# First feed-forward product: longer planned transfers, two raw buffers per matrix, relu stores issued by ScalarE, narrowing that begins on ScalarE

## The chip, the cores and the metric

One core of a Trainium2 chip. A core has TensorE (PE: matmuls; PEld is its loading of weights), VectorE (DVE), ScalarE (ACT), GpSimd (POOL) and SyncE (SP), each with a queue that runs in order, and 16 DMA engines that move data between HBM and the on-chip memory. Here nearly all transfers are issued from SP's queue. The metric is the time of one execution in device microseconds.

## The reference, cut to what matters

Attention (4 x 12 heads, 448 positions, 64 wide) feeds a gated convolution block, and that feeds a normalized feed-forward block; 4 x 448 = 1792 rows of 768 in all.

```python
xn = (x - mu) / np.sqrt(var + 1e-06) * g_ln
ch = np.maximum(xn @ w_ch1, 0.0) @ w_ch2     # 768 -> 3072 -> 768
return (x + ch).astype(np.float32)
```

`w_ch1` and `w_ch2` are float64 arrays. The kernel gets them as pairs of 32-bit words and narrows them to float32 on the chip.

## The kernel before, in words

**Phases.** Attention and gate come first (to about 254 us in the profile), then the output projection with the normalization (to about 355), then the first feed-forward product (355 to 737) and the second (from 737 to the end). The change lies in the first feed-forward product, in the two narrowings done ahead of it, and in the buffers that the second takes over.

**Precision.** Each float32 operand is split into a high part, rounded to the fast matmul type (F32R), and a low part, the rest. Each product is three matmuls: high x high, high x low, low x high.

**The first product.** `w_ch1` is cut into NJ = 24 column blocks of 128, the rows into NM = 4 row blocks (one of 256 rows, three of 512). A unit (j, m) is 18 matmuls into one of three PSUM banks (ring `c`). `ch1_products` (L589) issues them. Units run j by j; the last `LASTJ` blocks are run row block by row block instead. When a unit is done, `keep` (L880) has ScalarE write its relu into one of four buffers (`r1`), and a DMA stores that to `hd` in DRAM (L888, 96 stores).

**The weights of the first matrix.** `w1_steps` (L810) makes block j: load the raw words into ring `raw0` (one buffer), narrow them into `wt`, scale by `g_ln` (L240), ScalarE casts the high part into a slot of ring `w1` (five slots `blk`), VectorE subtracts to get the low part (L819). `first_steps` (L691) does the same for blocks 0 and 1 in the phase before.

**The second matrix beside it.** Its 24 raw pieces are narrowed in the same stretch, two per step, 12 steps in all (`w2_steps`, L828). The two pieces go from ring `raw1` (two buffers) into the one tile `comb`; four VectorE operations form sums and differences (L847), ScalarE casts the high parts into `combh` (L856), VectorE subtracts the low parts (L858), and two DMAs of 1344 KB store both tiles to `wd` in DRAM (L862, L863). The second product loads from `hd` and `wd` and takes over `X`, `blk`, `comb`, `combh`, `relu` and the raw buffers as space.

**Narrowing one piece** (`narrowing`, L791; 128 x 768 float64). Load (L792); three VectorE steps build the float32 bits from the two words (L220, L222, L224); ScalarE takes the absolute value of the high word, read as a float (L233), and writes it over the low word; a fourth VectorE step sets small values to zero (L236).

**What sets the order.** All of it is put in order before the kernel runs. `Plan.arrange` (L99) is a list scheduler: each task has a cost in ns on its engine, a `lag` after which its result is there (for DMAs), a due time, the tasks it comes after, and the buffers it takes. At any planned moment it starts, on each free engine, the earliest due among those tasks whose predecessors and buffers are ready; tasks are not held back until they are due. The result is one fixed order per engine. On the chip each engine runs its list in that order and waits, at the head of its queue, for whatever the next instruction needs. Planned costs of units are 4104 ns (512 rows) and 2160 ns (256 rows), `ENDB` is their sum. A block of the first matrix is due 22 us before its first unit, and 10 us before the next block.

The lines of the narrowing's load and of its due time:

```python
ld = task({"SP": 1500}, lambda e: nc.sync.dma_start(out=raw.tile, in_=src), due - 8,
          [raw_last[raw.tag], *need], [raw], lag=3000)
```

`need` is, for the second matrix, the last subtraction of the step before (`lo_last`).

Of the kernel before, what the change touches and what calls it, by code (L numbers as in the profile page):

```python
# [16 lines left out]

MIN_HIGH = 3.4332275390625e-05
# [139 lines left out]
def f32(ap):  # L158
    return ap.bitcast(F32)
# [3 lines left out]
def attention_gate_ffn(  # L163
# [71 lines left out]
    def narrow_2(raw, w):  # L235
        nc.vector.scalar_tensor_tensor(w, f32(raw[:, :, 0]), MIN_HIGH, w, ALU.is_ge, ALU.mult)  # L236

# [337 lines left out]
    NX = 2  # L575
# [6 lines left out]
    with ExitStack() as ph2:  # L582
# [13 lines left out]

        with ExitStack() as ph2a, tc.manual_schedule():
# [93 lines left out]
            def first_steps(n):  # L691

                raw, w, dst = Buf("wraw"), Buf("wt"), {}
# [3 lines left out]
                def bits(i):  # L697
                    def fn(e):
                        if i == 0:
                            dst["ops"] = narrow_ops(raw.tile, w.tile)  # L700
                        next(dst["ops"])
                    return fn

                k = ld
                for i, ns in enumerate((590, 990, 875)):
                    k = task({"DVE": ns}, bits(i), due + 0.01 * i, [k], [w] if i == 0 else [], [raw] if i == 0 else [raw, w])
                k = task({"ACT": 815}, lambda e: narrow_abs(raw.tile), due + 0.2, [k], [], [raw])
                def last(e):
                    narrow_2(raw.tile, w.tile)
                    scale_rows(w.tile)  # L710

                k = task({"DVE": 1740}, last, due + 0.3, [k], [], [raw, w])
# [15 lines left out]
        with ExitStack() as ph2b, tc.manual_schedule():  # L728
            bp = ph2b.enter_context(tc.tile_pool(name="bp", bufs=1, reuse_waits="tile"))
            ps_b = ph2b.enter_context(tc.tile_pool(name="ps_b", bufs=1, space=PSUM, reuse_waits="tile"))  # L730
            blk += [bp.tile([P, 2, DM], F32R, name=f"w1_{i}") for i in (2, 3, 4)]
            raws = [wr.tile([P, DM, 2], U32, tag="wraw", name="wraw")]
            raws += [bp.tile([P, DM, 2], U32, name=f"wraw{i}") for i in (1, 2)]
# [18 lines left out]
            def as_h(t, at):  # L752
# [3 lines left out]
                "raw0": raws[:1], "raw1": raws[1:], "w1": blk, "wt": [bp.tile([P, DM], F32, name="wt")], "comb": [comb], "combh": [combh],  # L756
# [5 lines left out]
                + [as_h(blk[s], i * NH) for s in (2, 3) for i in range(2)] + [as_h(X[3], 2 * NW + i * NH) for i in range(2)]  # L762
                + [as_h(blk[4], i * NH) for i in range(2)],
                "S": [cut(t, 0, 4 * JJ * P, i=4, j=JJ) for t in (comb, relu)],
                "r": [cut(f32(t), 0, 4 * JJ * P, f=2, j=JJ) for t in map(f32, raws)],
# [4 lines left out]
            LASTJ = 3  # L770
# [15 lines left out]
            w1_buf, w1_ready, w1_last, raw_last, lo_last = {}, {}, [None], {"raw0": None, "raw1": None}, [None]  # L786
# [4 lines left out]
            def narrowing(src, w_of, due, new, w_buf, raw, need=()):  # L791
                ld = task({"SP": 1500}, lambda e: nc.sync.dma_start(out=raw.tile, in_=src), due - 8, [raw_last[raw.tag], *need], [raw], lag=3000)  # L792
                raw_last[raw.tag] = ld
                dst = {}

                def bits(i):
                    def fn(e):
                        if i == 0:
                            dst["ops"] = narrow_ops(raw.tile, w_of())
                        next(dst["ops"])  # L800
                    return fn

                k = ld
# [277 lines left out]
```

## Time and profile before

| | |
|---|---|
| median of 3 runs | 1049.47 us (1048.47 to 1050.14) |
| profiled execution | 1049.6 us |
| its span, first to last instruction | 1047.9 us |
| TensorE busy in the span | 1004.5 us, 96 % |
| VectorE busy | 748.8 us, 71 % |
| ScalarE busy | 472.4 us, 45 % |
| GpSimd busy | 318.6 us, 30 % |
| TensorE clock, mean granted | 0.992 |
| moved by DMA | 193.76 MB |

How to read it: a busy share is a mean over the phases of the span, and TensorE's busy time is that of pipelined matmuls, so a busy engine may still run at the lower clock or wait to refill. What matters for a phase is which wait ends last there. Granted clock is that of TensorE, 1.00 being 2.4 GHz. In rows with "<-", the operation left of it waited for the one to its right; "SPq" and "ACTq" are the queues of SP and ScalarE, where DMA issues stand, which are not counted as busy. "Landing" is the time from a DMA's issue to its last data.

### The profile page before, as it was taken

Reading aid. Unit: us, or ns where it says so; the run is one execution under the profiler, and the core shown is the slowest. Engines: PE = TensorE matmul, PEld = TensorE weight load, DVE = VectorE, ACT = ScalarE, POOL = GpSimd, SP = SyncE. Lnnn points to the kernel's source line nnn. Section 1 sums busy time; section 2 is a strip of 40 time slices with the busy share of each in tenths; the row PEclk is TensorE's granted clock in tenths of the full one; section 3 lists DMA queues with packets and bytes.
Section 4 is the critical chain, followed back from the end, with each engine's and each line's share of the span. In section 5 each row is a group of like instructions: output and inputs, shape, how many; then the busy total and the mean of one; then the engine's idle time right before and its main releaser. Section 6 shows DMA issues by size and latency. Waiting matters only on the chain.

```text
span 1047.9 us, 16248 instructions
## 1 busy us (share of the span) xinstructions
PE 1004.5 (96%) x5947; PEld 882.5 (84%) x5947; DVE 748.8 (71%) x1361; ACT 472.4 (45%) x958; POOL 318.6 (30%) x389
## 2 busy tenths in 40 slices
PE   9989899999999999999988988899999999999998
PEld 5657677779999988878777876678999999999998
DVE  7898889763744467877767778761697787777773
ACT  8897878851554334434333343332333333333330
POOL 6979869560100000000000000001564443433510
PEclk9999999999999999999999999999999999999999
DMA  6354454332321367776777766679725616626422
GB/s 203 102 180 158 138 169 150 106 92 86 119 62 46 99 223 235 263 254 239 254 276 279 246 226 246 233 274 395 277 91 194 273 61 231 237 69 253 161 106 91
DMA packets 94127, 193.76 MB, mean 185 GB/s; under 512 B 8800, under 2 KB 75360, under 8 KB 90464
## 3 DMA queue, kind: packets, MB, share of 16 engines
q1 hardware_dynamic: 93904, 192.73, 52.4%
q8 instruction: 47, 0.77, 0.3%
q14 instruction: 32, 0.26, 0.1%
q10 hardware_dynamic: 144, 0.00, 0.0%
HBM read 126.65 MB, written 66.06 MB: 184 GB/s over the span
## 4 chain that ended last, share of the span: by engine, by line
PE 63%; DVE 17%; DMA 13%; POOL 3%; issue 2%; SPq 1%; ACT 0%; DVEq 0%; ACTq 0%; POOLq 0%
PE bank L998 23%; DMA wraw<-in_w_ch 13%; PE bank L594 12%; PE o L639 8%; PE val L554 5%; PE e L998 4%; PE t L399 2%; PE pv L423 2%; PE s L554 2%; DVE g L441 2%; DVE comb L847 2%; DVE wt L222 2%; PE s L328 2%; DVE wt L224 2%; POOL p L364 2%
## 5 line engine op out<-in xcount | busy, mean ns | idle before, releaser
L594 PE MATMUL bank<-x,w 128*128 128x512 f32 (+1 forms) x1692 | 355.5, 372 | 27.0 <-ACT relu L885 25.0
L594 PEld LDWEIGHTS bank<-x,w 128*128 128x128 f32 x1692 | 296.3, 192 | 85.8 <-ACT relu L885 31.3
L949 POOL TENSOR_TENSOR comb<-wraw 128x384 f32<-128x384 f32 x28 | 33.1, 1184 | 428.6 <-DMA hd<-relu 362.7
L1009 DVE TENSOR_TENSOR acc<-bank,acc 128x384 f32<-128x384 f32 x168 | 93.1, 554 | 71.7 <-PE bank L998 71.5
L998 PE MATMUL bank<-x,w 128*128 128x384 f32 x657 | 121.1, 334 | 0.0
L233 ACT ACTIVATE wraw<-wraw 128x768 f32<-128x768 f32 x60 | 55.6, 930 | 136.2 <-DVE comb L222 92.7
L998 PEld LDWEIGHTS bank<-x,w 128*128 128x128 f32 x657 | 114.5, 188 | 0.0
L364 POOL TENSOR_SCALAR p<-p,r 128x128 f32<-128x128 f32 (+1 forms) x144 | 78.1, 562 | 21.5 <-DVE r L360 13.8
L998 PE MATMUL bank<-x,x 128*128 128x384 f32 x432 | 81.6, 334 | 0.2 <-DVE acc L1009 0.2
L356 ACT ACTIVATE p<-p,negm 128x128 f32<-128x128 f32 (+1 forms) x144 | 71.8, 503 | 11.1 <-DVE negm L350 10.5
L998 PEld LDWEIGHTS bank<-x,x 128*128 128x128 f32 x432 | 75.4, 188 | 0.5 <-issue 0.5
L441 DVE SCALAR_TENSOR_TENSOR g<-pv,cw,g 128x444 f32<-128x444 f32 (+1 forms) x96 | 64.7, 674 | 10.9 <-POOL g L432 8.9
L885 ACT ACTIVATE relu<-bank 128x512 f32<-128x512 f32 (+1 forms) x94 | 48.9, 543 | 50.7 <-PE bank L594 36.2
L978 ACT CAST x<-wraw 128x384 fp32r<-128x384 f32 x69 | 35.3, 514 | 70.4 <-PE bank L998 33.9
L639 PE MATMUL o<-wo,yh 128*128 128x384 f32 x336 | 62.5, 339 | 0.0
L220 DVE TENSOR_SCALAR comb<-wraw 128x768 uint32<-128x768 uint32 x24 | 13.4, 559 | 67.2 <-DMA wraw<-in_w_ch 67.2
L949 POOL TENSOR_TENSOR relu<-wraw 128x384 f32<-128x384 f32 x28 | 34.4, 1228 | 84.3 <-DMA wraw<-hd 59.3
L639 PEld LDWEIGHTS o<-wo,yh 128*128 128x128 f32 x336 | 58.0, 188 | 0.0
L350 DVE CUSTOM_DVE_ANT_0 p<-s,mask 128x128 f32<-128x128 f32 (+1 forms) x144 | 51.9, 417 | 2.1 <-PE s L328 1.9
L979 DVE TENSOR_TENSOR x<-wraw,x 128x384 fp32r<-128x384 f32 x69 | 44.2, 644 | 6.7 <-ACT x L978 6.7
L554 PE MATMUL val<-xh,wvh 128*128 128x448 f32 x108 | 44.6, 413 | 1.6 <-DVE g L564 1.6
L979 DVE TENSOR_TENSOR w<-comb,w 128x384 fp32r<-128x384 f32 x41 | 37.9, 926 | 10.4 <-ACT w L978 10.4
(132 smaller groups left out, 1795.3 us busy)
## 6 DMA issues: line engine op xcount, KB each, us to landing
wraw<-in_w_ch SPq DMA_DIRECT2D x48, 768.0 KB, 9.7
x<-wd SPq DMA_DIRECT2D x22, 1152.0 KB, 7.0
wraw<-hd SPq DMA_DIRECT2D x28, 768.0 KB, 4.3
hd<-relu SPq DMA_DIRECT2D x72, 256.0 KB, 8.1
wd<-combh SPq DMA_DIRECT2D x12, 1344.0 KB, 7.7
wd<-comb SPq DMA_DIRECT2D x12, 1344.0 KB, 8.4
raw<-in_qk SPq DMA_DIRECT2D x24, 512.0 KB, 4.5
v<-in_v SPq DMA_DIRECT2D x24, 256.0 KB, 2.8
```

The source lines that it names most:

```text
L233: nc.scalar.activation(f32(raw[:, :, 0]), f32(raw[:, :, 1]), AF.Abs)
L350: nc.vector.tensor_tensor_reduce(buf.tile[:, o:o + w], bank.tile[:, at:at + w], m, NEG_SCALE, 3.0e38, ALU.add, ALU.min, negm.tile[:, i:i + 1])
L356: nc.scalar.activation(reg, reg, AF.Exp, bias=negm.tile[:, i:i + 1], scale=-1.0, accum_out=ssum.tile[:, i:i + 1])
L364: nc.gpsimd.tensor_scalar(reg, reg, r.tile[:, i:i + 1], 1.0, ALU.mult, ALU.mult)
L441: nc.vector.scalar_tensor_tensor(g.tile[:, d:], pv.tile[:, :S - d], cw[:, c, t:t + 1], g.tile[:, d:], ALU.mult, ALU.add)
L554: nc.tensor.matmul(ps.tile[:, :S], w[:, do, kc * P:(kc + 1) * P], x.tile, start=(kc == 0 and i == 0), stop=(kc == KC - 1 and i == 2),)
L594: nc.tensor.matmul(ps, w[:, a, kc], X[m][:, x, kc], start=(n == 0), stop=(n == 3 * KC - 1))
L639: nc.tensor.matmul(o.tile[:, nh, :HALF], y.tile[:, kc], wo_t[kc][:, a, nh * HALF:(nh + 1) * HALF], start=(count[nh] == 0), stop=(count[nh] ...
L949: nc.gpsimd.tensor_tensor(s.tile[:, o], a(), b(), op)
L979: k = task({"DVE": 556}, lambda e, src=src, h=h: nc.vector.tensor_tensor(h.tile[:, 1], src(), f32(h.tile[:, 0]), ALU.subtract), due + 1, [ ...
L998: nc.tensor.matmul(ps.tile[:, :HALF], h.tile[:, a, jj], w.tile[:, c, jj], start=(n == 0 and fresh), stop=(n == 3 * JJ - 1), skip_group_che ...
L1009: k = task({"DVE": 556}, lambda e, a=a: nc.vector.tensor_tensor(a, ps.tile[:, :HALF], a, ALU.add), t0 + UNIT + 0.2, [k], [], [ps])
```

## The change

1. In `narrowing`, the planned lag of a load goes from 3000 to 7000 ns and its due time from 8 to 16 us ahead of the narrowing; the second matrix's loads no longer come after `lo_last`. The planned lag of the stores to `wd` goes from 4500 to 7000 ns.
2. `raw0` and `raw1` get two buffers each (four raw tiles instead of three); ring `w1` has four slots instead of five.
3. The relu's store is issued by ScalarE (`nc.scalar.dma_start`), with a planned cost of 60 ns and a lag of 8000, in place of SP with 500 and 2500.
4. Narrowing: ScalarE writes the absolute value of the high word into the target tile first; VectorE then takes the maximum with 2^-15, shifts and masks in place, and merges low bits and sign bits in two more steps. The same order is used in `first_steps`. The phases before keep the old one.
5. `LASTJ` goes from 3 to 2; the due times of the second matrix's steps are spread over `ENDB - 55` instead of `ENDB - 75`; the second product's rings `h`, `S` and `r` take other tiles (`S`: `comb` and the fourth raw tile instead of `comb` and `relu`; `r`: three raw tiles and `relu` instead of three raw tiles).

```diff
+SMALL = 2.0 ** -15
+    def bits_of(raw, w):
+        wu = w.bitcast(U32)
+        high, low = raw[:, :, 1], raw[:, :, 0]
+        nc.vector.tensor_scalar(w, w, SMALL, SMALL, ALU.max, ALU.max)
+        yield
+        nc.vector.tensor_scalar(wu, wu, 3, 0x3FFFFFF8, ALU.logical_shift_left, ALU.bitwise_and)
+        yield
+        nc.vector.scalar_tensor_tensor(wu, low, 29, wu, ALU.logical_shift_right, ALU.bitwise_or)
+        yield
+        nc.vector.scalar_tensor_tensor(wu, high, 0xC0000000, wu, ALU.bitwise_and, ALU.bitwise_or)
+        yield
+
+    def magnitude(raw, w):
+        nc.scalar.activation(w, f32(raw[:, :, 1]), AF.Abs)
...
-            blk += [bp.tile([P, 2, DM], F32R, name=f"w1_{i}") for i in (2, 3, 4)]
+            blk += [bp.tile([P, 2, DM], F32R, name=f"w1_{i}") for i in (2, 3)]
-            raws += [bp.tile([P, DM, 2], U32, name=f"wraw{i}") for i in (1, 2)]
+            raws += [bp.tile([P, DM, 2], U32, name=f"wraw{i}") for i in (1, 2, 3)]
...
-                "raw0": raws[:1], "raw1": raws[1:], "w1": blk, ...
+                "raw0": raws[:2], "raw1": raws[2:], "w1": blk, ...
...
-                "S": [cut(t, 0, 4 * JJ * P, i=4, j=JJ) for t in (comb, relu)],
-                "r": [cut(f32(t), 0, 4 * JJ * P, f=2, j=JJ) for t in map(f32, raws)],
+                "S": [cut(t, 0, 4 * JJ * P, i=4, j=JJ) for t in (comb, f32(raws[3]))],
+                "r": [cut(f32(t), 0, 4 * JJ * P, f=2, j=JJ) for t in (*map(f32, raws[:3]), relu)],
...
-            LASTJ = 3
+            LASTJ = 2
...
-                ld = task({"SP": 1500}, ..., due - 8, [raw_last[raw.tag], *need], [raw], lag=3000)
+                ld = task({"SP": 1500}, ..., due - 16, [raw_last[raw.tag], *need], [raw], lag=7000)
...
-                for i, ns in enumerate((555, 990, 957)):
-                    n = new if i == 0 else []
-                    k = task({"DVE": ns}, bits(i), due + 0.01 * i, [k], n, [raw] if n else [raw, w_buf])
-                k = task({"ACT": 920}, lambda e: narrow_abs(raw.tile), due + 0.05, [k], [], [raw])
-                return task({"DVE": 957}, lambda e: narrow_2(raw.tile, w_of()), due + 0.1, [k], [], [raw, w_buf])
+                k = task({"ACT": 920}, lambda e: magnitude(raw.tile, w_of()), due, [ld], new, [raw] if new else [raw, w_buf])
+                for i, ns in enumerate((480, 480, 957, 957)):
+                    k = task({"DVE": ns}, bits(i, raw, w_of), due + 0.01 * (i + 1), [k], [], [raw, w_buf])
+                return k
...
-                return 10 + n * (ENDB - 75) / (NK * JJ - 1)
+                return 8 + n * (ENDB - 55) / (NK * JJ - 1)
...
-                    done.append(narrowing(..., due + 5 * f, [] if f else [cb], cb, raw, [lo_last[0]]))
+                    done.append(narrowing(..., due + 5 * f, [] if f else [cb], cb, raw))
...
-                    task({"SP": 2500}, ... out=wd[kk][:, :, 0, jj, :] ..., due + 2, his, [], [ch], lag=4500),
+                    task({"SP": 2500}, ... out=wd[kk][:, :, 0, jj, :] ..., due + 2, his, [], [ch], lag=7000),
...
-                k = task({"SP": 500}, lambda e: nc.sync.dma_start(out=dst, ...), due + 0.4, [k], [], [r1], lag=2500)
+                k = task({"ACT": 60}, lambda e: nc.scalar.dma_start(out=dst, ...), due + 0.2, [k], [], [r1], lag=8000)
```

## Rows read from the trace of the kernel before

**Rows 1.** The page: its first line, and the product's line among the costliest groups.
```profile
span 1047.9 us, 16248 instructions
...
L594 PE MATMUL bank<-x,w 128*128 128x512 f32 (+1 forms) x1692 | 355.5, 372 | 27.0 <-ACT relu L885 25.0
```

**Rows 2.** Table of windows over the first product: whole, first, middle, last stretch.
```profile
core 0: us, PE busy (x) PEld busy (x) DVE busy (x) ACT busy (x) POOL busy (x), PEclk, DMA share, GB/s
355.18:737.42 382.24, 355.27 (x1694) 296.37 (x1693) 259.53 (x305) 136.93 (x194) 5.63 (x5) 0.98 0.74 261
355.18:438.74 83.56, 83.56 (x410) 70.83 (x409) 59.93 (x73) 33.89 (x47) 0.00 (x0) 1.00 0.67 230
438.74:698.25 259.51, 232.54 (x1106) 192.71 (x1104) 188.92 (x221) 92.44 (x130) 0.00 (x0) 0.97 0.72 253
698.25:737.42 39.17, 39.17 (x181) 32.83 (x182) 10.69 (x13) 10.60 (x19) 5.63 (x5) 1.00 1.00 377
```

**Rows 3.** The same table for two windows of 4 us (PEclk: granted clock).
```profile
508.00:512.00 4.00, 3.08 (x14) 2.23 (x12) 1.64 (x3) 0.12 (x1) 0.00 (x0) 1.00 1.04 409
512.00:516.00 4.00, 2.89 (x7) 2.29 (x8) 3.47 (x5) 1.54 (x3) 0.00 (x0) 0.67 0.82 305
```

**Rows 4.** Waits in the first product: who for whom, us in total, times, longest.
```profile
ACT wraw L233 <- DVE comb L222: 92.7, 21, 8.2
DVE comb L220 <- DMA wraw<-in_w_ch: 67.2, 18, 6.7
...
DVE wt L220 <- DMA wraw<-in_w_ch: 15.8, 15, 7.2
```

**Rows 5.** Timeline from 498 us: start, duration, engine and line; idle before, releaser.
```profile
498.05 0.52 SPq L863 DMA_DIRECT2D wd<-comb  x1
498.62 1.44 SPq L792 DMA_DIRECT2D wraw<-in_w_ch  x1
...
500.15 3.82 SPq L888 DMA_DIRECT2D hd<-relu  x3
...
504.08 1.42 SPq L792 DMA_DIRECT2D wraw<-in_w_ch  x2
...
510.29 0.56 DVE L220 TENSOR_SCALAR comb<-wraw 128x768 uint32<-128x768 uint32 x1 [6.17 <-DMA wraw<-in_w_ch]
...
511.88 0.92 ACT L233 ACTIVATE wraw<-wraw 128x768 f32<-128x768 f32 x1 [6.39 <-DVE comb L222]
...
512.69 0.85 ACT L885 ACTIVATE relu<-bank 128x256 f32<-128x256 f32 x2
...
513.11 7.17 PE L594 MATMUL bank<-x,w 128*128 128x512 f32 x28 [2.02 <-ACT relu L885]
```

**Rows 6.** By source line: relu stores; later big stores, their landing; the loads' landing.
```profile
L888 SPq DMA_DIRECT2D hd<-relu x96: 320/412/2208, 356.3 to 738.1; - x96
...
L863 SPq DMA_DIRECT2D wd<-comb x12: 512/519/520, 380.7 to 705.2; - x12
...
DMA to landing us min/median/max: 7.6/8.4/8.8
...
DMA to landing us min/median/max: 4.2/9.8/11.8
```

**Rows 7.** SP's own waits in the first product.
```profile
SPq L888 <- ACT relu L885: 193.9, 50, 27.3
SPq L792 <- DVE wt L236: 33.5, 10, 5.1
```

**Rows 8.** Timeline of ScalarE at the kernel's start: its one transfer issue.
```profile
0.89 0.38 ACTq L490 DMA_DIRECT2D g_t<-in_g_ln  x1
```

**Rows 9.** Groups by line in the product: count, busy us, mean ns, idle before.
```profile
L233 ACT ACTIVATE wraw<-wraw 128x768 f32<-128x768 f32 x46 | 42.6, 931 | 136.2 <-DVE comb L222 92.7 <-DVE wt L222 43.0 <-ACT relu L885 0.5
...
L222 DVE SCALAR_TENSOR_TENSOR comb<-wraw,comb 128x768 uint32<-128x768 uint32 x24 | 23.0, 958 | 0.7
...
L220 DVE TENSOR_SCALAR comb<-wraw 128x768 uint32<-128x768 uint32 x24 | 13.4, 559 | 67.2 <-DMA wraw<-in_w_ch 67.2
```

More of the change, by code (lines that the diff above doesn't have):

```diff
@@ L595, in ch1_products, with bits, fn @@
                     n += 1
+        def bits(i, raw, w_of):
+            def fn(e):
+                if i == 0:
+                    raw.ops = bits_of(raw.tile, w_of() if callable(w_of) else w_of.tile)
+                next(raw.ops)
+            return fn
         with ExitStack() as ph2a, tc.manual_schedule():
@@ L691, in first_steps @@
             def first_steps(n):
-                raw, w, dst = Buf("wraw"), Buf("wt"), {}
+                raw, w = Buf("wraw"), Buf("wt")
                 due = 0.6 + 2.6 * n
                 ld = task({"SP": 3800}, lambda e: nc.sync.dma_start(out=raw.tile, in_=w1_b[n]), due - 1, new=[raw], lag=2500)
[L697 to L712, printed above, removed]
+                k = task({"ACT": 920}, lambda e: magnitude(raw.tile, w.tile), due, [ld], [w], [raw])
+                for i, ns in enumerate((480, 480, 957, 957)):
+                    k = task({"DVE": ns}, bits(i, raw, w), due + 0.01 * (i + 1), [k], [], [raw, w])
+                k = task({"DVE": 957}, lambda e: scale_rows(w.tile), due + 0.3, [k], [], [w])
                 k = task({"ACT": 740}, lambda e: cast_hi(blk[n][:, 0], w.tile, nc.scalar), due + 0.4, [k], [], [w])
@@ L841, in w2_steps @@
                     raw_bufs.append(raw)
-                    done.append(narrowing(w2_b[kk * 2 * JJ + f * JJ + jj], piece(f), due + 5 * f, [] if f else [cb], cb, raw, [lo_last[0]]))
+                    done.append(narrowing(w2_b[kk * 2 * JJ + f * JJ + jj], piece(f), due + 5 * f, [] if f else [cb], cb, raw))
                 due += 5.5
@@ L868, in attention_gate_ffn @@
                 w1_buf[j], w1_ready[j] = pre[j], None
-            plan.before["w1"] = [*pre, Buf("w1")]
+            plan.before["w1"] = pre
             steps = [(w1_due[j], w1_steps, j) for j in range(NX, NJ)]
@@ L887, in keep @@
                 dst = hd[kk][us, :, f, jj, :].rearrange("u p n -> p u n")
-                k = task({"SP": 500}, lambda e: nc.sync.dma_start(out=dst, in_=r1.tile[:, :n].rearrange("p (u n) -> p u n", n=2 * P)),
-                         due + 0.4, [k], [], [r1], lag=2500)
+                k = task({"ACT": 60}, lambda e: nc.scalar.dma_start(out=dst, in_=r1.tile[:, :n].rearrange("p (u n) -> p u n", n=2 * P)),
+                         due + 0.2, [k], [], [r1], lag=8000)
                 for u in range(us.start, us.stop):
@@ L905, in attention_gate_ffn @@
             last_c = {i % 3: c for i, c in enumerate(c_bufs)}
-            slot = {(j + (j >= NX)) % 5: w1_buf[j] for j in range(NJ)}
+            slot = {j % len(blk): w1_buf[j] for j in range(NJ)}
             def past(bufs):
```

30 lines of the change are left out of this document (11 added, 19 removed).

## The prediction

> **What bounds the kernel now.** I read the page first: TensorE is busy nearly all of the span, and the line with the largest idle time ahead of it is the first feed-forward product [rows 1]. Next the table of windows over that product, from its first matmul at 355.18 us to its last at 737.42 us [rows 2]. It holds three stretches. In the first 83.56 us and the last 39.17 us TensorE is busy without a gap at granted clock 1.00. In the 259.51 us between them it is busy 232.54 us, so 26.97 us idle, at a mean clock of 0.97. All of the loss lies in that middle stretch.
>
> How long would the product take with no stall? The plan prices a block of 512 columns at 4.104 us and the short block of 256 at 2.160 us. The last stretch tests that price: its 180 matmuls (the row counts one more, cut by its edge) are nine long blocks and one short one, 9 x 4.104 + 2.160 = 39.10 us, and it took 39.17 [rows 2]. The whole product has 24 x 3 long and 22 short blocks, 72 x 4.104 + 22 x 2.160 = 343.0 us. It took 737.42 - 355.18 = 382.24 us. So 39.2 us are lost: 27.0 idle, and 12.2 in busy time that is longer than the work.
>
> Part of those 12.2 us is the clock. In the instance below TensorE stands idle from 511.09 to 513.11 us: the window of 4 us in which that begins has the clock 1.00, the next 0.67, a mix of the levels 2.4 and 1.2 GHz [rows 3]. A mean of 0.97 over 259.51 us lacks 0.03 x 259.51 = 7.8 us of work at full clock; the remaining 4 us I put down to draining and refilling.
>
> Who ends the stalls? TensorE waits for the relu that empties its bank, 25.0 of 27.0 us [rows 1]; ScalarE waits for VectorE's bit steps (92.7 us for the second matrix) and VectorE for the loads of raw weights (67.2 and 15.8 us) [rows 4]. One instance shows the chain whole [rows 5]. At 498.62 the first load of a second-matrix step is issued; three stores of relu results stand behind it on SP from 500.15 to 503.97, and only at 504.08 come the next loads. The data of the first arrive so late that VectorE's step on it starts at 510.29 after 6.17 us idle. ScalarE's abs waits for VectorE until 511.88; the relu queued behind it runs at 512.69; TensorE gets its bank at 513.11, after 2.02 us idle. So no engine is full (VectorE 259.53 of 382.24, ScalarE 136.93 [rows 2]): orders on the queues are made with transfers that are planned at 4.5 us (1500 ns of issue and 3000 of lag), and they take 9.8 [rows 6].
>
> **The change part by part.**
> *Load times, raw buffers, priority.* The planned load becomes 8.5 us and that of the big stores 7.0 becomes 9.5 us, against medians of 9.8 for loads and 8.4 for the later big store [rows 6]. The first matrix gets a second raw buffer, and the second's loads no longer come after the previous step's last subtraction. SP waits 33.5 us for VectorE to free a raw buffer [rows 7]. One block of the first matrix comes about every 14.5 us (3 x 4.104 + 2.160), so a load into a second buffer can be issued about a block ahead, and even the slowest of 11.8 us [rows 6] lands in time. What hides the load is now that lead; without it 9.8 us per load would be bare again. No transfer is added.
>
> *Stores to ScalarE.* 96 stores leave SP. SP stood 193.9 us behind relus with them [rows 7]; loads and big stores no longer queue behind that. ScalarE pays. Its one transfer issue in the trace took 0.38 us [rows 8]; on SP the same store has a minimum of 0.32, a median of 0.41 and a maximum of 2.21 [rows 6]. I take 0.41, the same instruction's median, plus 0.10 for the overlap that the next instruction loses (the relu at 512.69 begins 0.11 before the abs of 511.88 + 0.92 ends [rows 5]): 96 x 0.51 = 49 us, against 6 us in the plan. ScalarE then has 137 + 49 = 186 us in about 348. Behind a store stand abs, casts and the next relu; a relu may come about two blocks late (three banks), 6.2 to 8.2 us, so half a microsecond stalls nobody. Ends: 96 x 0.32 = 31 us and 96 x 2.21 = 212 us; ScalarE would then hold 349 us, the slow rival below. No gain on ScalarE is possible, since it issued none of them.
>
> The rows say that SP lost time by waiting, not by issuing. The Trainium skill (DMA: Bandwidth & Descriptors, "Issuing engines are not separate DMA queues") speaks against the move: transfers from several engines run on the same 16 DMA engines, and only the sequencer's time of issue is saved, usually small. By it the move would be worth 96 x 0.41 = 39 us of SP's time and nothing of the kernel's; what it would then give is the third rival.
>
> *Narrowing.* Per matrix piece, old: 0.559 + 3 x 0.957 = 3.43 us on VectorE, the abs of 0.93 between its third and fourth step [rows 9]. New: the abs first, at the same 0.93, then maximum and shift, each a step like the one at 0.559, then two of 0.957: 3.03 us. 46 pieces x 0.40 = 18 us less VectorE work, beside TensorE's, so nothing off the end directly. If the two cheap steps took 0.957, it is 46 x 0.40 = 18 us more (VectorE 278 of 343, still not full); if 0.48, as planned, 26 us less. The new wait: the abs waits for the load itself and for the target tile, so for the landing of the earlier big store; relus and casts stand behind it and TensorE waits for those. Today ScalarE reaches the same load through VectorE, so this wait replaces one, it does not add one. The two pieces narrowed before the product lie beside a TensorE that is not waiting: nothing.
>
> *The second matrix's cycle.* It now runs from one tile's freeing to the next. Twelve later stores are issued from 380.7 to 705.2 us: a period of 324.5 / 11 = 29.5 us [rows 6]. In the instance, 498.05 (store issued) to 510.29 (first step on the next data) is 12.2 us [rows 5]; the new order needs there the store's issue and landing, 0.52 + 8.4 = 8.9, so 3.3 less; two pieces save 0.8 on VectorE and the abs at the head adds 0.93. About 26.3 us; twelve make 316, inside 343. It becomes late only beyond some 28.
>
> *Fewer first-matrix slots (4), last group of 2, other buffers at the turn.* A slot is needed again after about 43 us (three blocks of 14.5), a block is made in some 14.5. The tiles in which the second product's first weights land come free 8 to 25 us before the turn instead of 12 to 37, a transfer takes up to 11.8 [rows 6] and the last of the seven is needed about 14 us after it. Nothing, with up to 5 us if the transfers pile up; the last stretch, where they do today, moves 377 GB/s without stalling TensorE [rows 2].
>
> **Sum.** 39.2 us can be had. I keep 5 us of loss: twelve second-matrix steps at 0.4, one store's issue each that falls into a burst of ScalarE work. The first 83.56 us, which already run at full speed, say 0 to that [rows 2]. The profiled execution took 1049.6 us (span 1047.9, 1.7 around it), 0.1 over the median 1049.47: 1049.6 - 39.2 + 5.2 = 1015.6, so **1016 us**.
>
> **The rivals.**
> *Half the stalls stay (0.16):* the abs at the head of ScalarE's order waits for loads and stores that land late, as VectorE's first step does now. For it: 67.2 of the 83.0 us that VectorE waits for loads are for this matrix [rows 4]. Against: two buffers and longer planned times. Half of 39.2 kept: 1030, between 1024 and 1038.
> *ScalarE becomes the bound (slower, 0.09):* it is the issue of stores on ScalarE, in the first product. ScalarE's work is 137 us, and its abs now waits 136.2 us more [rows 9]. Suppose half of that, 68, stays in its order. It then decides from 137 + 68 + 96 x s = 382, s = 1.8 us a store, on. At the 2.21 that a store on SP reaches [rows 6] the product takes 417 us, 35 more than now, and the kernel 1085. Against: the median of 0.41 and the one issue of 0.38 [rows 8]. The Trainium skill (Perfetto Trace Analysis, "DMA Instruction — HWDGE") has issuing sequencers lock one shared descriptor generator, which speaks for it; no row here has two issuers at once.
> *The change does not bring the loads forward (same, 0.04):* the transfers are the limit, whoever issues them. For it: windows of share 1.00 and more in bursts [rows 3]. Against: 0.74 of 382.24 us is 283 us of transfers, less than 343 [rows 2]. It would give 1049.
>
> **How the numbers follow.** Forecast with its own range 1010 to 1024: 0.68. The three rivals: 0.16, 0.09, 0.04; 0.03 is left for a smaller gain, 1038 to 1047. The range 1010 to 1038 holds 0.84: below it nothing is left to gain, above it stands what I leave out. Measurement tells 0.2 % (2.1 us) from no change: faster 0.68 + 0.16 + 0.03 = 0.87, same 0.04, slower 0.09.
>
> **What would show it.** Right: the product takes 343 to 352 us, TensorE's idle time for relu falls from 25 us below 6 and the clock stays at 1.00; VectorE's wait for loads almost vanishes; store issues on ScalarE last about 0.41 us; maximum and shift about 0.5; later big stores come every 26 to 28 us, and the second product starts without a gap. Wrong: abs of the second matrix waiting long for loads or landed stores with relus behind it; issues above 1 us; or a second product that waits for its first sums.

## The result and the profile after

| | before | after |
|---|---|---|
| median | 1049.34 us (1048.47 to 1050.14) | 1009.42 us (1009.36 to 1009.73) |
| ratio to before, 95 % interval | | 0.9620 (0.9604 to 0.9637) |
| profiled execution, its span | 1049.6, 1047.9 us | 1009.73, 1007.9 us |
| first feed-forward product | 382.24 us | 341.72 us |
| what lies ahead of it, what lies behind it in the span | 355.18 and 310.5 us | 357.00 and 309.2 us |

The change takes 39.9 us off. The forecast was 1016 us in a range from 1010: the sign and the mechanism held, the gain was 6.6 us larger than forecast, and the time lies 0.6 us below the range.

The page of the changed kernel, its first line and the lines of the product (L610 is the old L594; the columns are count, busy us, mean ns, idle before):

```profile
span 1007.9 us, 16212 instructions
...
L610 PE MATMUL bank<-x,w 128*128 128x512 f32 (+1 forms) x1692 | 342.0, 364 | 0.0
...
L884 ACT ACTIVATE relu<-bank 128x512 f32<-128x512 f32 (+1 forms) x94 | 51.1, 543 | 113.3 <-PE bank L610 109.5
```

Where 27.0 us of idle time stood [rows 1] there is none. The chain that ended last, in order of time (start, duration, what), has the whole product as one piece of TensorE with all 1692 matmuls:

```profile
357.00 341.72 PE bank L610 x1692
```

The windows over the product, to be read against [rows 2]: whole, and its parts. The granted clock is 1.00 throughout, so the half-speed stretches of [rows 3] went with the stalls.

```profile
357.00:698.72 341.72, 341.72 (x1693) 290.70 (x1693) 247.24 (x309) 141.26 (x196) 12.73 (x12) 1.00 0.83 291
357.00:440.00 83.00, 83.00 (x405) 70.26 (x405) 66.14 (x83) 36.53 (x50) 0.00 (x0) 1.00 0.74 256
440.00:660.00 220.00, 220.00 (x1104) 187.63 (x1103) 175.87 (x219) 95.47 (x128) 0.00 (x0) 1.00 0.85 296
660.00:698.72 38.72, 38.72 (x189) 32.81 (x188) 5.22 (x8) 9.27 (x18) 12.73 (x12) 1.00 0.88 335
```

The DMA engines' work is what it was: 0.83 x 341.72 = 284 us, against 0.74 x 382.24 = 283 before. It is squeezed into less time, no less of it. VectorE's work falls from 259.53 to 247.24 us, ScalarE's rises from 136.93 to 141.26, issues not counted.

The waits in the product (who for whom, total us, times, longest) against [rows 4]:

```profile
ACT relu L884 <- PE bank L610: 109.5, 48, 3.7
...
ACT comb L252 <- DMA wd<-comb: 21.8, 9, 6.4
...
ACT comb L252 <- DMA wraw<-in_w_ch: 11.9, 8, 2.0
```

ScalarE now waits for TensorE, not the other way round. The loads that cost VectorE 83.0 us now cost ScalarE 11.9 us, and its longest single wait is the new one, up to 6.4 us for the store of the tile to land (21.8 us in 9 waits). None of them reaches TensorE.

The stores and loads by source line, against [rows 6]: the relu store on ScalarE's queue; the later big store and its landing; the loads' landing.

```profile
L887 ACTq DMA_DIRECT2D hd<-relu x96: 336/366/1503, 358.2 to 699.4; - x96
...
L862 SPq DMA_DIRECT2D wd<-comb x12: 513/518/520, 387.8 to 659.2; - x12
...
DMA to landing us min/median/max: 8.9/10.0/13.4
...
DMA to landing us min/median/max: 4.1/7.3/14.8
```

A store costs ScalarE 0.37 us (median; at most 1.50). The later big stores come every (659.2 - 387.8) / 11 = 24.7 us, where they came every 29.5, although each takes 10.0 us to land instead of 8.4. Loads take 7.3 us by the median, but up to 14.8.

The narrowing by groups, against [rows 9]:

```profile
L252 ACT ACTIVATE comb<-wraw 128x768 f32<-128x768 f32 x24 | 21.7, 907 | 34.1 <-DMA wd<-comb 21.8 <-DMA wraw<-in_w_ch 11.9 <-ACT relu L884 0.4
...
L244 DVE TENSOR_SCALAR comb<-comb 128x768 uint32<-128x768 uint32 x24 | 13.4, 560 | 0.8
L242 DVE TENSOR_SCALAR comb<-comb 128x768 f32<-128x768 f32 x24 | 13.3, 555 | 12.6 <-ACT comb L252 12.5
```

Maximum and shift take 0.555 and 0.560 us, as the old shift did.

### The profile page after: what moved, and what is told of

It is laid out like the page before. It is cut to its first block, busy times and chain, and to the rows that moved or that the text cites. A ratio compares the mean times of both kernels' runs of the same rounds, so it can differ in the third digit from the quotient of the medians.

```text
span 1007.9 us, 16212 instructions
## 1 busy us (share of the span) xinstructions
PE 990.9 (98%) x5947; PEld 877.2 (87%) x5947; DVE 717.1 (71%) x1361; ACT 476.7 (47%) x958; POOL 314.7 (31%) x389
## 4 chain that ended last, share of the span: by engine, by line
PE 90%; DVE 6%; POOL 3%; issue 1%; ACT 0%; ACTq 0%; POOLq 0%; DVEq 0%
PE bank L610 34%; PE bank L997 26%; PE o L662 9%; PE val L570 5%; PE e L997 4%; PE t L415 2%; PE pv L439 2%; PE s L570 2%; DVE g L457 2%; PE s L344 2%; POOL p L380 2%; DVE p L366 1%; PE x L704 1%; PE s L319 1%; PE pv L444 1%
## 5 line engine op out<-in xcount | busy, mean ns | idle before, releaser
L610 PE MATMUL bank<-x,w 128*128 128x512 f32 (+1 forms) x1692 | 342.0, 364 | 0.0
L610 PEld LDWEIGHTS bank<-x,w 128*128 128x128 f32 x1692 | 290.6, 189 | 50.9
L997 PE MATMUL bank<-x,x 128*128 128x384 f32 x549 | 101.9, 334 | 0.0
L997 PEld LDWEIGHTS bank<-x,x 128*128 128x128 f32 x549 | 95.8, 188 | 0.0
L997 PE MATMUL bank<-x,w 128*128 128x384 f32 x486 | 90.7, 334 | 0.0
L997 PEld LDWEIGHTS bank<-x,w 128*128 128x128 f32 x486 | 84.8, 188 | 0.0
L380 POOL TENSOR_SCALAR p<-p,r 128x128 f32<-128x128 f32 (+1 forms) x144 | 78.1, 563 | 21.4 <-DVE r L376 13.1
L372 ACT ACTIVATE p<-p,negm 128x128 f32<-128x128 f32 (+1 forms) x144 | 71.8, 502 | 11.3 <-DVE negm L366 10.7
L978 DVE TENSOR_TENSOR x<-wraw,x 128x384 fp32r<-128x384 f32 x75 | 51.3, 685 | 26.6 <-ACT x L977 23.5
L415 PEld LDWEIGHTS t<-ident,p 128*128 128x128 f32 x288 | 32.6, 140 | 14.5 <-ACT pt L418 4.9
L415 PE MATMUL t<-ident,p 128*128 128x128 f32 x288 | 42.1, 278 | 2.7 <-ACT pt L418 1.9
L418 ACT COPY pt<-t 128x512 f32<-128x512 f32 x72 | 39.4, 580 | 9.4 <-PE t L415 9.1
L689 POOL TENSOR_TENSOR rs<-rs,mhalf 128x1 f32<-128x1 f32 x14 | 9.6, 686 | 109.4 <-DVE rs L684 109.4
```

What stands on the lines that cost most here:

```text
L372: nc.scalar.activation(reg, reg, AF.Exp, bias=negm.tile[:, i:i + 1], scale=-1.0, accum_out=ssum.tile[:, i:i + 1])
L380: nc.gpsimd.tensor_scalar(reg, reg, r.tile[:, i:i + 1], 1.0, ALU.mult, ALU.mult)
L415: nc.tensor.transpose(bank.tile[:, j * P:(j + 1) * P], buf.tile[:, o:o + P], ident)
L610: nc.tensor.matmul(ps, w[:, a, kc], X[m][:, x, kc], start=(n == 0), stop=(n == 3 * KC - 1))
L978: k = task({"DVE": 556}, lambda e, src=src, h=h: nc.vector.tensor_tensor(h.tile[:, 1], src(), f32(h.tile[:, 0]), ALU.subtract), due + 1, [ ...
L997: nc.tensor.matmul(ps.tile[:, :HALF], h.tile[:, a, jj], w.tile[:, c, jj], start=(n == 0 and fresh), stop=(n == 3 * JJ - 1), skip_group_che ...
```

## The experiments

Six groups: one part undone; one part alone; the buffers with one more part; one raw buffer by itself; ScalarE loaded on purpose; and the two narrowings ahead of the product. Medians are of three rounds beside the kernel before on the same chip; ratios are to that. "Times" means planned transfer times, with the loads' earlier due time and the lifted order of the second matrix's loads, which were not tried apart; "buffers" means raw tiles, slots, last group, rings and due times of the second matrix's steps.

| kernel | us | ratio to before (95 %) |
|---|---|---|
| after, stores back on SP | 1009.88 | 0.9610 (0.9595 to 0.9624) |
| after, old narrowing in the product | 1013.70 | 0.9647 (0.9629 to 0.9666) |
| after, first matrix with one raw buffer | 1026.05 | 0.9751 (0.9736 to 0.9765) |
| after, old buffers | 1048.40 | 0.9980 (0.9970 to 0.9989) |
| after, old times | 1056.40 | 1.0054 (1.0037 to 1.0071) |
| before, new buffers | 1026.39 | 0.9777 (0.9762 to 0.9791) |
| before, new narrowing | 1048.82 | 0.9969 (0.9954 to 0.9984) |
| before, new times | 1054.58 | 1.0046 (1.0032 to 1.0060) |
| before, stores on ScalarE | 1059.72 | 1.0081 (1.0065 to 1.0097) |
| before, times and buffers | 1013.44 | 0.9655 (0.9641 to 0.9669) |
| before, buffers and stores on ScalarE | 1038.34 | 0.9870 (0.9853 to 0.9888) |
| before, buffers and narrowing | 1045.08 | 0.9937 (0.9921 to 0.9952) |
| after, one relu more per store | 1010.82 | 0.9607 (0.9591 to 0.9623) |
| after, three relus more per store | 1044.16 | 0.9925 (0.9910 to 0.9940) |
| after, old narrowing ahead of the product | 1008.78 | 0.9611 (0.9597 to 0.9626) |

### One part undone

**Stores back on SP.**

```diff
-                k = task({"ACT": 60}, lambda e: nc.scalar.dma_start(out=dst, ...), due + 0.2, [k], [], [r1], lag=8000)
+                k = task({"SP": 500}, lambda e: nc.sync.dma_start(out=dst, ...), due + 0.2, [k], [], [r1], lag=8000)
```

> The changed kernel with one part undone: the relu stores are issued by SP again (planned cost 500 ns, the new lag of 8000 kept). Theory 1 (the orders were made with transfer times too short, and right times cure it): 1009 to 1013 us, TensorE's wait for relu below 2 us. Theory 2 (loads stood behind stores on SP, and only a queue of their own for the stores cures it): 1025 us or more, SP again waiting over 100 us for relus, TensorE waiting over 10 us. Theory 3 (the second raw buffer gives the lead): 1009 to 1013.

1009.88 us. SP's own waits in the product (same columns as [rows 7]):

```profile
SPq L887 <- ACT relu L884: 162.1, 68, 6.6
```

SP stands behind relus nearly as long as before, 162.1 us instead of 193.9, and it costs nothing. Theory 2 falls here: with times and buffers right, the stores need no queue of their own.

**Old times.**

```diff
-                ld = task({"SP": 1500}, ..., due - 16, [raw_last[raw.tag], *need], [raw], lag=7000)
+                ld = task({"SP": 1500}, ..., due - 8, [raw_last[raw.tag], *need], [raw], lag=3000)
...
-                    done.append(narrowing(..., due + 5 * f, [] if f else [cb], cb, raw))
+                    done.append(narrowing(..., due + 5 * f, [] if f else [cb], cb, raw, [lo_last[0]]))
...
-                    task({"SP": 2500}, ..., due + 2, his, [], [ch], lag=7000),   # and the other big store
+                    task({"SP": 2500}, ..., due + 2, his, [], [ch], lag=4500),
...
-                k = task({"ACT": 60}, ..., lag=8000)
+                k = task({"ACT": 60}, ..., lag=2500)
```

> The changed kernel with the planned transfer times undone: loads at a lag of 3000 ns and due 8 us ahead, stores of both matrices at 4500, relu stores at 2500 (still issued by ScalarE), the second matrix's loads again after the last subtraction of the step before. Theory 1 (times): 1025 us or more, TensorE waiting over 10 us for relus. Theory 2 (queue) and theory 3 (raw buffers): 1009 to 1014 us.

1056.40 us, slower than before. Its waits, and a stretch of its timeline (start, duration, engine and line; idle before, releaser):

```profile
ACT comb L252 <- DMA wraw<-in_w_ch: 100.2, 21, 11.2
...
PE bank L610 <- ACT relu L885: 30.7, 15, 5.9
```

```profile
501.74 0.89 ACT L252 ACTIVATE comb<-wraw 128x768 f32<-128x768 f32 x1 [5.96 <-DMA wraw<-in_w_ch]
502.53 0.59 ACT L885 ACTIVATE relu<-bank 128x512 f32<-128x512 f32 x1
...
503.17 19.05 PE L610 MATMUL bank<-x,w 128*128 128x512 f32 x84 [2.68 <-ACT relu L885]
```

Here is the prediction's first rival at work: the abs of the second matrix waits 5.96 us for its load at the head of ScalarE's order, the relu behind it comes at 502.53, and TensorE has stood 2.68 us. With the rest of the change in place, the new times are needed.

**Old buffers.**

```diff
-            blk += [... for i in (2, 3)]
+            blk += [... for i in (2, 3, 4)]
-            raws += [... for i in (1, 2, 3)]
+            raws += [... for i in (1, 2)]
-                "raw0": raws[:2], "raw1": raws[2:], ...
+                "raw0": raws[:1], "raw1": raws[1:], ...
-            LASTJ = 2
+            LASTJ = 3
-                return 8 + n * (ENDB - 55) / (NK * JJ - 1)
+                return 10 + n * (ENDB - 75) / (NK * JJ - 1)
...
```

(The rings of the second product and the numbering of the slots go with it.)

> The changed kernel with the buffers undone: three raw tiles (one for the first matrix, two for the second), five slots for the first matrix, last group of 3, the second product's old rings, the old due times of the second matrix's steps. Theory 3 (raw buffers): 1025 us or more, with VectorE or ScalarE waiting over 40 us for loads. Theories 1 and 2: 1009 to 1014 us.

1048.40 us. The relus are served, but the blocks of the first matrix are late. What TensorE waits for, and the longest of its stops (a second, of 8.93 us, comes below):

```profile
PE bank L610 <- ACT w L214: 21.4, 3, 9.1
PE bank L610 <- DVE w L819: 6.5, 7, 1.4
```

```profile
693.53 0.79 PE L610 MATMUL bank<-x,w 128*128 128x256 f32 x2 [9.05 <-ACT w L214]
```

Theory 3's time is right, its reason is not: I expected waits of over 40 us for loads, and ScalarE waits 6.9 us for them (4.1 and 2.8). The way to the stop of 8.93 us (same columns):

```profile
663.79 0.96 DVE L248 SCALAR_TENSOR_TENSOR wt<-wraw,wt 128x768 uint32<-128x768 uint32 x1
...
664.83 13.57 SPq L803 DMA_DIRECT2D wraw<-in_w_ch  x2
...
673.16 0.89 ACT L252 ACTIVATE wt<-wraw 128x768 f32<-128x768 f32 x1
...
679.61 0.79 PE L610 MATMUL bank<-x,w 128*128 128x256 f32 x2 [8.93 <-ACT w L214]
```

The one raw buffer is free when the last step on it ends at 664.75. Only then can the next load be issued, its abs runs at 673.16, and the block is there at 679.61. One buffer puts the load and the narrowing behind each other, some 15 us for a block, and the last group of three wants its blocks faster than that.

**Old narrowing in the product.**

```diff
-                k = task({"ACT": 920}, lambda e: magnitude(raw.tile, w_of()), due, [ld], new, ...)
-                for i, ns in enumerate((480, 480, 957, 957)):
-                    k = task({"DVE": ns}, bits(i, raw, w_of), ...)
-                return k
+                for i, ns in enumerate((555, 990, 957)):
+                    k = task({"DVE": ns}, bits(i), ...)
+                k = task({"ACT": 920}, lambda e: narrow_abs(raw.tile), ...)
+                return task({"DVE": 957}, lambda e: narrow_2(raw.tile, w_of()), ...)
```

> The changed kernel with the old narrowing in the first product (three bit steps on VectorE, abs on ScalarE, fourth step on VectorE); the two narrowings ahead of the product stay new. All three theories: no stall comes back, 1009 to 1012 us, VectorE's busy time in the product up by 46 x 0.40 = 18 us less what the abs steps gain. A fourth theory (the head on ScalarE shortens the second matrix's cycle and that is what counts): 1020 us or more.

1013.70 us (1011.89 to 1015.84), 3.8 us more than the stores back on SP on the same chip, and 1.7 us above what all three theories allowed. The product itself is untouched, no idle time. The loss is at the turn, where TensorE waits for a weight transfer of the second product (1.3 us in the profiled execution, which at 1011.89 was the shortest of the four). The last of the later big stores is issued at 684.3 us instead of 659.2.

```profile
PE e L1008 <- DMA x<-wd: 1.3, 1, 1.3
```

```profile
L873 SPq DMA_DIRECT2D wd<-comb x12: 514/524/527, 387.7 to 684.3; - x12
```

The weights that TensorE waits for are not those of the last store: the second product's first seven transfers need only the first three steps, stored long before. What comes late is space: GpSimd writes the second product's first sum into the tile `comb`, which the last store frees, and the next weight transfers into `x` are issued some 12 us later. First the kernel with the stores back on SP, then this one (start, duration, engine and line; idle before, releaser):

```profile
667.17 1.01 POOL L948 TENSOR_TENSOR comb<-wraw 128x384 f32<-128x384 f32 x1 [313.49 <-DMA wd<-comb]
683.72 0.41 SPq L935 DMA_DIRECT2D x<-wd  x1
```

```profile
694.88 1.01 POOL L959 TENSOR_TENSOR comb<-wraw 128x384 f32<-128x384 f32 x1 [341.24 <-DMA hd<-relu]
695.86 6.74 SPq L946 DMA_DIRECT2D x<-wd  x4
```

In the first the profile names the landing of that store as the releaser; in the second it names a relu's store that landed about when the big one did (684.3 + 10.3 = 694.6), so that the big store held it there is argued, not shown.

So the new narrowing is worth some 4 us after all, where the second matrix must be finished. Whether by its work or by its order was not parted: the later big stores come every (684.3 - 387.7) / 11 = 27.0 us here and every 24.7 in the changed kernel, and only 0.8 us of that difference is VectorE's saved work on two pieces. The fourth theory has the shorter cycle right, and not its price.

Of the three theories, 1 and 3 both hold in the changed kernel, and neither alone: with right times the old buffers leave nothing of the gain, with the new buffers the old times. As theory 5 this went into the next runs.

### One part alone, on the kernel before

The edits are those above, the other way round, on the kernel before (the relu stores' lag goes with the times, except where the stores are on ScalarE at the old lag).

> The kernel before with the new planned transfer times alone (loads, both big stores, relu stores, the second matrix's loads no longer after the last subtraction); stores stay on SP, old buffers, old narrowing. Theory 5, from the four runs with a part undone (right times and the second raw buffer are needed together, neither does anything alone): 1040 to 1060 us, the stalls now for blocks of the first matrix that are not ready rather than for relus. Theory 1 (right times alone are the cure): 1015 us or less.

1054.58 us: slower than before by 0.46 %. Theory 1 alone falls. The stalls change their kind, as theory 5 held: TensorE waits for blocks of the first matrix and no longer for relus.

```profile
PE bank L594 <- ACT w L213: 24.9, 11, 7.7
PE bank L594 <- DVE w L819: 6.1, 12, 0.9
```

> The kernel before with the new buffers alone (two raw tiles per matrix, four slots, last group of 2, new rings and due times of the second matrix's steps); old times, stores on SP, old narrowing. Theory 5: 1040 to 1060 us, TensorE waiting over 15 us for relus. Theory 3 (buffers alone are the cure): 1015 us or less.

1026.39 us. Theory 5 falls in its strong form: the buffers alone give 2.2 % with the old times, more than half of the gain. TensorE waits 13.1 us for relus instead of 25.0.

> The kernel before with times and buffers together; stores stay on SP, old narrowing in and ahead of the product. Theory 5: 1008 to 1015 us, the stores' queue and the new narrowing being worth at most 4 us together. A theory in which the store on ScalarE or the new narrowing also carries a large part: 1020 us or more.

1013.44 us, 3.45 % below before. The product has no idle time (its 1692 matmuls take 342.0 us busy, 0.0 idle). What is left to the changed kernel is the turn:

```profile
PE bank L998 <- DVE w L979: 1.9, 1, 1.9
...
PE e L998 <- DMA x<-wd: 1.0, 1, 1.0
```

> The kernel before with the relu stores issued by ScalarE alone, at the old lag. The prediction held that loads standing behind the stores on SP is one cause of the stalls (theory 2): 1040 us or less. Theory 6 (the orders' wrong times and the raw buffers, not SP's queue): 1045 to 1060 us.

1059.72 us, 0.81 % slower than before: theory 6, theory 2 falls for good. SP no longer waits for relus with its stores; its loads now wait for VectorE to free a raw buffer (126.5 us) and behind earlier loads (88.2), and TensorE waits 34.2 us for relus.

```profile
SPq L792 <- DVE wt L236: 126.5, 18, 11.8
SPq L792 <- DMA wraw<-in_w_ch: 88.2, 10, 10.0
```

> The kernel before with the new narrowing in the product alone; old times, old buffers, stores on SP. Theory 6: 1055 us or more, slower than before, since the abs waits for loads at the head of ScalarE's order. If the 18 us less work on VectorE count in a product that stalls: 1040 us or less.

1048.82 us, 0.31 % below before: neither expectation. The abs at the head waits 80.7 us for the second matrix's loads, as theory 6 held, and TensorE 25.5 us for relus, as before. So with the old buffers the abs at the head is no loss even though the loads are late; what makes up for its wait was not parted.

### Buffers and one more part, with the old times

> The kernel before with the new buffers and the new narrowing in the product; old times, stores on SP. Buffers alone gave 1026 us, the changed kernel with old times 1056. Theory 6 (with loads planned too short, the abs at the head of ScalarE's order waits for late loads with relus behind it, and this costs some 30 us): 1045 us or more, ScalarE's abs waiting over 60 us for loads. If it is the store on ScalarE that did it: 1022 to 1030 us.

1045.08 us: theory 6, at its limit. The new narrowing, which costs nothing with right times, takes the ratio from 0.978 to 0.994 here, 1.6 %. ScalarE's abs waits:

```profile
ACT comb L252 <- DMA wraw<-in_w_ch: 93.4, 23, 9.9
...
PE bank L610 <- ACT relu L897: 24.4, 12, 5.0
```

> The kernel before with the new buffers and the relu stores issued by ScalarE at the old lag; old times, old narrowing. With the new buffers alone 1026 us, with buffers and new narrowing 1045, with all three (changed kernel, old times) 1056. Theory 6 (the abs at the head of ScalarE's order is what makes wrong times dear, and the store adds the rest): 1026 to 1037 us. If the store makes them as dear as the abs: 1045 us or more.

1038.34 us, 1.3 us above theory 6's range. With the old times the store on ScalarE costs 0.9 % beside the new buffers, the narrowing 1.6 %; all three together are at 1.0054, 2.8 % above the buffers alone. The two costs about add.

### The first matrix's second raw buffer by itself

The changed kernel without it:

```diff
-                "raw0": raws[:2], "raw1": raws[2:], ...
+                "raw0": raws[:1], "raw1": raws[2:], ...
```

> The changed kernel with one thing of the buffers undone: the first matrix has one raw buffer instead of two (slots, last group and rings stay new). If that buffer is what made the kernel with all buffers undone fall back to 1048 us: 1030 us or more, TensorE waiting over 15 us for blocks of the first matrix. If it is the slots, the last group or the due times: 1009 to 1015 us.

1026.05 us, between the two expectations: this buffer alone is worth 1.3 % (0.962 to 0.975) of the 3.6 % that undoing all buffers costs. TensorE stops 11.3 us for blocks of the first matrix, 7.12 of them once, at 684.47 us. The rest lies in what was undone beside it (slots, last group, due times); which of these was not tried.

### ScalarE loaded on purpose

```diff
+                def stored(e):
+                    nc.scalar.activation(r1.tile[:, :n], r1.tile[:, :n], AF.Relu)   # once, or three times
+                    nc.scalar.dma_start(out=dst, ...)
-                k = task({"ACT": 60}, lambda e: nc.scalar.dma_start(out=dst, ...), ...)
+                k = task({"ACT": 60}, stored, ...)
```

> The changed kernel with the relu computed once more, in place, ahead of each of the 96 stores on ScalarE (0.59 us for 512 columns, unknown to the plan). The price of a store on ScalarE so rises by about 0.55 us; ScalarE's work from 141 to about 194 us plus the issues. By the term of the sum that kept 5 us of loss (one store's time lost in each of twelve bursts): 12 x 0.55 = 7 us more, 1016 us. By slack (three banks leave a relu some 6 us, nothing is lost until ScalarE is full): 1009 to 1011 us.

1010.82 us, a ratio no higher than the changed kernel's: slack. ScalarE does 54 us more work, and the product takes 341.74 us, as without it.

```profile
357.00:699.00 342.00, 342.00 (x1699) 291.05 (x1698) 247.24 (x309) 195.44 (x291) 11.82 (x12) 1.00 0.83 291
```

```profile
357.82 341.74 PE bank L610 x1692
```

> The same with three more relus per store: ScalarE's work 141 + 3 x 52 = 297 us plus 36 us of issues, 333 of the product's 342 us. By slack alone, nothing lost until ScalarE is full: 1009 to 1020 us. By the rival in which half of ScalarE's waiting stays in its order, the bound is passed (1.8 us a store; here 0.4 + 1.65 = 2.0): 1050 us or more.

1044.16 us, between the two. TensorE waits 21.6 us for relus. ScalarE's 304.91 us of work in these 375 leave out 96 issues (0.37 us each, 36 us, by the changed kernel's median): some 341, as long as the undisturbed product. The product takes 371 us (from its first matmul at 357.18 to the second product's first at 728.27), so some 30 us of ScalarE's waiting stayed. With 195 us of work nothing was lost, with 341 some 33 (against 1010.82 on the same chip); where between the loss begins was not tried.

```profile
357.00:732.00 375.00, 352.74 (x1714) 293.70 (x1712) 246.67 (x309) 304.91 (x485) 12.18 (x12) 1.00 0.77 268
```

```profile
PE bank L610 <- ACT relu L884: 21.6, 21, 2.5
```

### The two narrowings ahead of the product

The changed kernel's one new stop of TensorE, and the ScalarE instructions around it:

```profile
268.36 0.87 PE L704 MATMUL x<-ident,xn 128*128 128x128 f32 x6 [1.78 <-ACT xn L696]
```

```profile
266.61 0.80 ACT L679 COPY acc<-o 128x768 f32<-128x768 f32 x1 [1.21 <-PE o L662]
267.31 1.00 ACT L696 ACTIVATE xn<-o,nm,rs 128x768 f32<-128x768 f32 x1
```

A copy that waits for TensorE (266.61) now stands ahead of the normalization (267.31) that TensorE waits for.

```diff
-                k = task({"ACT": 920}, lambda e: magnitude(raw.tile, w.tile), due, [ld], [w], [raw])     # first_steps
...
+                for i, ns in enumerate((590, 990, 875)):
+                    k = task({"DVE": ns}, bits(i), due + 0.01 * i, ...)                                   # as before
...
```

> The changed kernel with the old narrowing in the two pieces ahead of the product only. In the changed kernel TensorE stood 1.78 us for a normalized tile at 268.36 us, behind a copy that ScalarE now does first. If the new order of these two pieces is what moved that copy: 1.8 us less, 1007.6 us (1007.0 to 1008.2), the product starting at about 355.2 instead of 357.0. If it comes from elsewhere: 1009.4.

1008.78 us (1008.30 to 1009.76), outside both expectations: the stop is gone, but of 1.8 us only 0.6 arrived, and the ranges of the two kernels overlap. In the profiled execution nothing arrived, the product starts at 357.00 in both: each tile of the output projection takes 0.11 us longer, 6.36 instead of 6.25, though its matmuls are the same, and twelve of them make up 1.3 us. The same 6.36 stands in the two kernels of before that have the stores on ScalarE (alone, and with the buffers), and 6.25 in all the others, some of them on the same chips. So it comes with the program, not with the chip; why stays open. This is the lowest median of all, not a version that clearly beats the changed kernel.

```profile
267.88 6.36 PE o L662 x36
```

```profile
269.23 6.25 PE o L662 x36
```

## Why the prediction was right or wrong

**The diagnosis of the stalls: right.** TensorE's 27.0 us of idle time and the half-speed stretches were put down to relus that came late (25.0 of 27.0 us), and both vanished together. That planned times too short make them late was only half of the cause: new times alone gain nothing.

**The size: the kept loss failed.** I kept 5.2 us, "twelve second-matrix steps at 0.4" (which is 4.8; the sum gives no reason for the other 0.4). Measured: 0. The step mistook an engine's delay for TensorE's. A relu had some 6 us of room, as the prediction's own part on the store says, and a delay of half a microsecond in a burst does not use that up. One relu more per store shows it: 54 us more on ScalarE, nothing lost in the product. The row that said 0, the first 83.56 us without a stall [rows 2], was read and not followed.

**The floor of the range: too high.** Without the kept loss the forecast is 1010.4, still inside the range; what carries the time below 1010 is the floor's own error. I let the range begin at 1010 because "below it nothing is left to gain". Two terms were missing. The blocks take 341.72 us, not 343.0, so the plan's price that I had tested on one stretch of 39.17 us is 0.4 % high. And the second product takes 309.2 us instead of 310.5; before, the chain of waits ran over VectorE from 745 to 767 us there. Against these, 1.8 us were lost ahead of the product. From the forecast of 1015.6: -5.2 (kept loss), -1.3 (price), -1.3 (second product), +1.8 (ahead) give 1009.6; the profiled execution took 1009.73.

**SP's queue: wrong as a cause.** In the instance I read the stores that stood ahead of the next loads as part of the delay. But the late load itself was issued at 498.62, ahead of those stores [rows 5], and landed 11.6 us later: they did not delay it. I weighed the Trainium skill's rule (DMA: Bandwidth & Descriptors, "Issuing engines are not separate DMA queues") against 193.9 us of waiting on SP [rows 7]. For this move the rule was nearer: with the stores back on SP the kernel takes 1009.88 us (not told apart from 1009.42), and moving them alone makes it 0.8 % slower. A queue's waiting was no loss here where nothing behind it was urgent; with right times and a buffer in hand, the loads were not. My third rival, that the whole change would then do nothing, does not follow from it, because the gain came from elsewhere.

**"This wait replaces one, it does not add one": wrong with late loads, right with early ones.** With the old times the abs at the head of ScalarE's order costs 1.6 % beside the new buffers; ScalarE reaches the load directly and the relus wait behind it. Beside the old buffers it cost nothing even so (1048.82 against 1051.90 for the kernel before on that chip), and with right times it costs nothing. So the first rival's mechanism was real, and in the changed kernel the planned times are what keeps it out: with old times it is at 1056.40.

**What made the gain: the mechanism with both parts was right, the split was not given.** Buffers alone give 2.2 %, times alone cost 0.5 %, together they give 3.45 % of the 3.8 %. Times with all the old buffers only move the stall, from relus to blocks of the first matrix. Of the buffers, the first matrix's second raw tile is worth 1.3 % by itself; the rest was not parted. The forecast treated them as one part, and so could not say that.

**The narrowing: the work right, its worth wrong.** Two steps at 0.555 and 0.560 us (forecast 0.559 each). "Nothing off the end directly" holds within the product; at the turn it is some 4 us (1013.70 against 1009.88 on one chip), where the second matrix is finished 25 us later without it. The cycle comes every 24.7 us (forecast 26.3), although a landing takes 10.0 us where I put 8.4; so the rest of the cycle is shorter than I allowed for, by which of its steps was not parted. The Trainium skill's advice to make the loads early and wait late (DMA: Bandwidth & Descriptors, "Rules for kernel authors") agrees: loads take up to 14.8 us here and TensorE does not notice.

**The store's price: right, at 0.37 us** (forecast 0.41); with the stores back on SP it is 0.37 there too. The slow rival needed 1.8. Its point was tested: at 0.37 + 3 x 0.57 = 2.1 us a store the kernel takes 33.3 us more than with one relu added. Work of 341 us fills most of it, and some 30 us of waiting stayed in ScalarE's order, less than half of the 68 that the rival kept. So its mechanism is there, at a price that the change does not reach.

**The two narrowings ahead: "nothing" was wrong by 1.8 us**, a copy that changed places with a normalization. Such a shift in a planned order could not be read from the trace of before.

## What to carry to other kernels

Where orders are planned ahead, planned transfer times and buffers belong together: with honest times and the old buffers the work came too late, with two buffers and times too short a late load still held up the queue. The buffers alone gave 2.2 of the 3.8 %, the times alone cost 0.5. A step moved to the head of another engine's order makes that engine wait for the transfer; here that cost 1.6 % beside the new buffers while the transfers came late, and nothing once they came early. A delay on an engine with slack, behind several buffers, can cost nothing at all, and here the cured stall was cured whole: the range has to reach down to the bare work, with the price of that work taken from an undisturbed stretch and the phases beside it counted too.

## What the runs showed of the hardware

The changed kernel and the one with its stores back on SP differ in the relu stores' issuer and in what the plan makes of it. Issues and landings, first of the changed kernel's relu stores (its big stores' landing stands above), then of the relu stores and the later big stores with SP alone:

```profile
DMA to landing us min/median/max: 1.7/6.2/12.1
```

```profile
L887 SPq DMA_DIRECT2D hd<-relu x96: 327/370/3542, 358.3 to 699.6; - x96
...
DMA to landing us min/median/max: 1.7/5.3/10.6
...
DMA to landing us min/median/max: 8.0/8.3/10.9
```

The issue costs 0.37 us by the median on either engine. With two issuers the relu stores land after 6.2 us and the later big stores after 10.0; with SP alone after 5.3 and 8.3. The kernel's time is the same (1009.42 and 1009.88 us). Whether the second issuer or the changed order makes the landings later was not parted. The total of transfer time is nearly the same, 0.83 x 341.72 = 284 us and 0.84 x 341.74 = 287, as the Trainium skill's rule on shared DMA engines (DMA: Bandwidth & Descriptors, "Issuing engines are not separate DMA queues") would have it.

And matmuls of the same shape ran 3 ns apart between kernels (339 and 342 ns in the output projection, the second in three of the kernels), for no reason that these runs show.
